# Decay attention and gated convolution on one core: the rows of q, kT and the state are told by the sequence instead of the head's parity

## The chip, the core and the metric

The kernel runs on one core of one Trainium2 chip. The metric is device time in microseconds of one execution; lower is better. A core has TensorE (PE; its weight loads are listed apart as PEld), VectorE (DVE), ScalarE (ACT), GpSimd (POOL) and SyncE (SP), which issues the transfers here. SBUF has 128 partitions; TensorE writes its products to the banks of PSUM.

## The reference

Two layers follow each other. The first is linear attention with a decay `lam` for each head, computed in blocks; the second gates a linear layer by a short causal convolution:

```python
# B=4 sequences, H=8 heads, S=768 tokens, D=64; block = 64
for b in range(nb):
    intra = einsum('bhic,bhjc->bhij', qb, kb) * Dmask       # lam^(i-j) for i >= j, else 0
    intra = einsum('bhij,bhjd->bhid', intra, vb)
    inter = einsum('bhid,bhde->bhie', qb * lam_pow, kv_state)
    out[:, :, sl] = intra + inter
    kv_state = lam_block * kv_state + einsum('bhsd,bhse->bhde', kb * rev_pow, vb)
# x = out as (B, S, 512)
gate = sigmoid(sum_k conv_w[k] * xp[:, k:k+S])              # 5 taps, causal
return (gate * (x @ w_val)) @ w_out
```

`q`, `k`, `v` and `lam` are fp32; `w_val`, `conv_w` and `w_out` come as 64-bit numbers, which the kernel turns into fp32 (the two matrices into pairs of rounded numbers, `_hi` and `_lo`) on the chip.

## The kernel before

The work is cut into twelve steps `i`. A step takes two of the four sequences (`NB2`, index `b`) and 128 tokens (`C`; the decay lets the block be larger than the reference's). Steps 0 to 5 run through the tokens of sequences 0 and 1, steps 6 to 11 through those of 2 and 3. Heads are numbered `h = 2 g + hh`: `g` from 0 to 3, `hh` the parity.

Each step does, in the names of the code:

- `plan_load` (L321): two transfers of 1 MB, one for each sequence, with q and k transposed (`qT`, `kT`: rows are the 64 dimensions of the heads, the upper 64 partitions for even heads and the lower 64 for odd ones) and v and k by tokens.
- `scale_k` (L399): k times the decay to the block's end, on ScalarE for steps in `K_ACT`, else on GpSimd. `scale_q` (L416): q times the decay from the block's start, on GpSimd.
- `scores` (L449) and `mask` (L466), for each `b`: kT times q on TensorE, and the result times `dmask` on VectorE, into `A`. There is one slot of two PSUM banks for scores (`s`); steps in `S_OWN` take two general banks for their second half.
- `inter` (L503): the state times the scaled q, sixteen 64 by 64 products with 128 columns, into `xp` (one slot of two banks, one bank for each `b`). `state[r, b, g, :]` has the rows of its head's parity, and the result goes to the partitions of the same parity, so a product sits on one of two diagonal 64 by 64 tiles of TensorE's array.
- `intra` (L519): v times `A`, added into `xp`.
- `outer` (L560), `update` (L573), `fade` (L579): the new state on TensorE, VectorE and GpSimd.
- `keep` (L619), `split_x` (L641), `split_x_lo` (L649): `xp` to SBUF, and its split into `x_hi` and `x_lo`. For steps in `X_DVE` the split is read from PSUM, with VectorE for `x_lo`.
- once in two steps, for four groups of channels: `tap` (L673), one on ScalarE and four on VectorE, and `sigmoid` (L689).
- `value` (L713), `apply` (L732), `split_h` (L752), `project` (L776), `store` (L792): the two linear layers with weights in two parts. Steps from `DIRECT` on multiply the gate straight from PSUM; earlier ones copy the product to SBUF first.

Steps 9, 10 and 11 (`STACK`) have no `inter`. There the first 64 keys and the state are stacked into one stationary operand of 128 rows (`vs`, filled by a transfer of `vh` and a copy of the state on ScalarE), with the moving operand stacked alike in `A` (half masked scores, half scaled q). The other 64 keys follow in `rest_of_keys` (L542): sixteen 64 by 64 products with 64 columns. Masks there are four VectorE instructions for a half step, and `scale_q` two on GpSimd.

The order on each engine is fixed at build time by `Plan` (L46). Each piece of work is added with an engine, a cost in ns, what it follows, the buffers that it holds and a rank. `Plan.order` simulates the engines, and an engine that is free takes the ready piece with the lowest rank whose buffers have a free slot (`SLOTS`). On TensorE a change of the tile mode costs `SWITCH`, and work of the present mode is preferred by `NEAR`. `RANK` sets how far each stage runs ahead or behind. PSUM has four general banks (`u`), which `value`, `project`, `outer` and the taps' sums share.

Of the kernel before, what the change touches and what calls it, by code (L numbers as in the profile page):

```python
# [9 lines left out]
F32 = mybir.dt.float32  # L10
# [13 lines left out]
SLOTS = {"ld": 3, "qd": 2, "A": 2, "x": 3, "xs": 2, "g": 2, "val": 4, "hs": 2, "o": 2, "s": 1, "xp": 1, "u": 4, "vs": 1}  # L24
UNIT = 2

K_ACT = (0, 1, 2, 3, 4)
X_DVE = (0,)
# [3 lines left out]

STACK = (9, 10, 11)
SWITCH = 130
OVER = {"DVE": 60, "ACT": 85, "POOL": 45}
NEAR = 0.6
# [96 lines left out]
def decay_attention_then_gated_conv(  # L133
# [3 lines left out]
    vh: bass.AP,  # L137
# [7 lines left out]
    B, NC = qkv.shape[0], qkv.shape[1]  # L145
    S = NC * C
    D = P // 2
    NP = qkv.shape[4] // C
    H = 2 * NP
    DM = H * D  # L150
# [6 lines left out]
    UC = HU * P  # L157
    PSUM = bass.MemoryType.PSUM
# [18 lines left out]

    swapped = const.tile([P, P], F32, name="swapped")
    for lo in (0, D):
        nc.gpsimd.tensor_copy(swapped[:, lo : lo + D], ident[:, D - lo : P - lo])  # L180
# [11 lines left out]
    lam_hd = const.tile([P, NP], F32, name="lam_hd")  # L192
# [6 lines left out]
    own_rows = lambda hh: slice(hh * D, (hh + 1) * D)  # L199
    other_rows = lambda hh: slice(D - hh * D, P - hh * D)  # L200
    sdec = const.tile([P, NB2, NP, D], F32, name="sdec")
# [6 lines left out]
    def make_dmask():  # L208
        for hh in range(2):
            for g in range(NP):  # L210
                nc.vector.tensor_tensor_scan(
                    out=dmask[:, hh, g, :],
                    data0=lam_bc[:, 2 * g + hh : 2 * g + hh + 1].to_broadcast([P, C]),
                    data1=ident if hh else swapped,
                    initial=0.0,
                    op0=ALU.mult,
                    op1=ALU.add,
                )

    def make_qdec(g):  # L220
        if g == 0:
            lam_v = lam_bc.rearrange("p (g hh) -> p hh g", hh=2)
            nc.vector.tensor_copy(lam_hd[0:D], lam_v[0:D, 0])
            nc.vector.tensor_copy(lam_hd[D:P], lam_v[D:P, 1])
        nc.vector.tensor_tensor_scan(
            out=qdec[:, g, :],
            data0=lam_hd[:, g : g + 1].to_broadcast([P, C]),
            data1=zero,
            initial=1.0,
            op0=ALU.mult,  # L230
            op1=ALU.add,
        )

    t_dmask = add("DVE", 5500, make_dmask, rank=-4)
# [86 lines left out]
    def plan_load(i):  # L321
        pair, c = divmod(i, NC)
        ld_buf[i] = Buf("ld")
        for b in range(NB2):


            cuts = (0, 2, 4) if i == 0 else (0, 4)
            for lo, hi in zip(cuts, cuts[1:]):

                def go(i=i, lo=lo, hi=hi, b=b, src=qkv[NB2 * pair + b, c]):  # L330
                    if i not in lds:
                        t = buf("ld", "ld", [P, NB2, 4, DM])
                        lds[i] = {
                            "all": t,
                            "qT": t[:, :, 0].rearrange("p b (g i) -> p b g i", g=NP),
                            "kT": t[:, :, 1].rearrange("p b (g i) -> p b g i", g=NP),
                            "v": t[:, :, 2],
                            "k": t[:, :, 3],
                        }
                    nc.sync.dma_start(lds[i]["all"][:, b, lo:hi], src[:, lo:hi])  # L340

                t_ld[i, b, hi] = add(
                    "DMA", 630 * (hi - lo), go, [], [ld_buf[i]],
                    i * RANK["ld"] + 0.01 * b + (-10 + 0.1 * lo if i == 0 else 0), lag=2300,
                )
            t_ld[i, b, 2] = t_ld[i, b, cuts[1]]
# [41 lines left out]
    t_state = t_sdec = t_x = t_vs = None  # L388
    vs = {}
# [3 lines left out]
    for i in range(N):  # L393
# [5 lines left out]
        def scale_k(i=i):  # L399
            kv = lds[i]["k"].rearrange("p b (g hh d) -> p hh g b d", hh=2, d=D)  # L400
            for hh in range(2):
                if i in K_ACT:
                    for g in range(NP):
                        nc.scalar.mul(kv[:, hh, g], kv[:, hh, g], dmask[:, hh, g, C - 1 : C])  # L404
                else:
                    for b in range(NB2):
                        nc.gpsimd.tensor_tensor(
                            out=kv[:, hh, :, b], in0=kv[:, hh, :, b],
                            in1=dmask[:, hh, :, C - 1 : C].to_broadcast([P, NP, D]),
                            op=ALU.mult,  # L410
                        )

        stacked = i in STACK
        A_buf = {b: Buf("A") for b in range(NB2)}

        def scale_q(b, i=i, s=s, stacked=stacked):  # L416
            if stacked:
                s["A", b] = buf("A", "A", [P, 2, NP, C])
                for hh in range(2):
                    r = own_rows(hh)  # L420
                    nc.gpsimd.tensor_tensor(
                        out=s["A", b][r, hh], in0=lds[i]["qT"][r, b], in1=qdec[r], op=ALU.mult
                    )
                return
            if b == 0:
                s["qd"] = buf("qd", "qd", [P, NB2, NP, C])
            nc.gpsimd.tensor_tensor(out=s["qd"][:, b], in0=lds[i]["qT"][:, b], in1=qdec, op=ALU.mult)  # L427

        t_kd = None
        t_qd = {}  # L430
        qd_buf = Buf("qd")
        if not last:
            t_kd = add(
                *(("ACT", 3150) if i in K_ACT else ("POOL", 2500)), scale_k,
                [t_ld[i, 0, 4], t_ld[i, 1, 4], t_dmask], [ld_buf[i]], R + RANK["kd"], port=i not in K_ACT, name=f"kd{i}",
            )
        if not first:
            for b in range(NB2):
                t_qd[b] = add(
                    "POOL", 2550 if stacked else 1300, lambda b=b, f=scale_q: f(b), [t_ld[i, b, 2], t_qdec, t_qd.get(0)],  # L440
                    [ld_buf[i], A_buf[b] if stacked else qd_buf], R + RANK["kd"], port=True, name=f"qd{i}",
                )

        t_mask = {}
        for b in range(NB2):
            own = b == 1 and i in S_OWN
            s_bufs = [Buf("u"), Buf("u")] if own else [Buf("s")]

            def scores(i=i, b=b, s=s, own=own, stacked=stacked):  # L449
                t = lds[i]  # L450
                if own:
                    s["s"] = [bank("so", [P, NP, C]) for hh in range(2)]
                else:
                    sp = bank("s", [P, 2, NP, C], "s")
                    s["s"] = [sp[:, 0], sp[:, 1]]
                    s["sp"] = sp
                for g in range(NP):
                    for hh in range(2):
                        r = slice(hh * D, (hh + 1) * D)
                        nc.tensor.matmul(  # L460
                            s["s"][hh][:, g, :], t["kT"][r, b, g, :], t["qT"][r, b, g, :],
                            start=True, stop=True,
                        )
                s["s", b] = s["s"] if own or stacked else s["sp"]

            def mask(b=b, s=s, own=own, stacked=stacked):  # L466
                if stacked:

                    if "A2" not in s:
                        s["A2"] = buf("qd", "A2", [P, NB2, NP, D])  # L470
                    for hh in range(2):
                        r = other_rows(hh)
                        nc.vector.tensor_tensor(  # L473
                            out=s["A", b][r, hh], in0=s["s", b][hh][r], in1=dmask[r, hh], op=ALU.mult
                        )
                    for hh in range(2):
                        r = own_rows(hh)
                        nc.vector.tensor_tensor(  # L478
                            out=s["A2"][r, b], in0=s["s", b][hh][r, :, D:], in1=dmask[r, hh, :, D:], op=ALU.mult
                        )  # L480
                    return
                s["A", b] = buf("A", "A", [P, 2, NP, C])
                if own:
# [369 lines left out]
```

## Time and profile before

| what | before |
|---|---|
| time, median of 3 runs | 237.28 us (235.39 to 237.3) |
| the profiled execution | 237.42 us, its span 235.6 us |
| TensorE busy | 222.2 us (94%) |
| VectorE, ScalarE, GpSimd busy | 155.5, 120.4, 141.1 us |
| bytes moved | HBM read 30.17 MB, written 6.29 MB |

The span runs from the first to the last instruction. "Busy" is the time in which an engine works on some instruction; the ends of TensorE's records are modelled, so they overlap a little. The chain of waits goes back from the last instruction, at each step to what released it. A timeline row gives start, length, engine, line, operation, operands and how many instructions it merges. One product of fp32 operands makes two records on TensorE and two on PEld.

### The profile page before, as it was taken

To read this page: it belongs to the slowest core of one execution; us is meant where nothing else is said; L and a number is where in the kernel's file an instruction comes from. 1 tells how busy PE (TensorE), PEld (TensorE's weight loads), DVE (VectorE), ACT (ScalarE), POOL (GpSimd) and SP (SyncE) were. 2 spreads that over 40 slices of the span, in tenths; PEclk is the share of its full clock that TensorE was granted. 3 is DMA by queue.
4 is the path that set the end of the run, shared out by engine and by line. 5 is a ranking of instruction groups with operands and counts; after the bars stand their busy time and mean duration, and the time that the engine had idled before them with its cause. 6 is when DMAs were issued, how large, how long until landed. Compare 5 with 4: busy or idle time off the path is not lost.

```text
span 235.6 us, 5414 instructions
## 1 busy us (share of the span) xinstructions
PE 222.2 (94%) x2302; PEld 198.0 (84%) x2302; DVE 155.5 (66%) x211; ACT 120.4 (51%) x200; POOL 141.1 (60%) x120
## 2 busy tenths in 40 slices
PE   7978999889799999999999979999999899999994
PEld 6967789779699999997778869898899799999984
DVE  4777798999998588840899799859811794111110
ACT  2385998735237636653675733866425373322222
POOL 1064899978693796999997946456125243522220
PEclk9999999999999999999999999999999999999999
DMA  5999999987430808009132121110111101111112
GB/s 159 419 420 423 419 419 419 309 312 331 199 161 11 344 18 345 3 13 359 76 92 89 45 89 47 40 53 3 47 45 50 64 22 45 55 62 62 48 46 89
DMA packets 9096, 36.81 MB, mean 156 GB/s; under 512 B 1264, under 2 KB 2288, under 8 KB 5744
## 3 DMA queue, kind: packets, MB, share of 16 engines
q1 hardware_dynamic: 9072, 36.47, 40.0%
q8 instruction: 18, 0.29, 0.5%
q14 instruction: 6, 0.05, 0.1%
HBM read 30.17 MB, written 6.29 MB: 155 GB/s over the span
## 4 chain that ended last, share of the span: by engine, by line
PE 65%; DVE 18%; DMA 8%; ACT 5%; issue 2%; SPq 0%; ACTq 0%; DVEq 0%
PE op L782 28%; PE vp L721 26%; DVE acc L685 9%; DMA ld<-in_qkv 8%; PE s L460 5%; DVE A L489 3%; PE xp L525 3%; DVE g L734 2%; PE xp L510 2%; PE st L567 2%; DVE A L473 1%; ACT ld L404 1%; DVE w_e L257 1%; DVE w_m L290 1%; DVE A L478 1%
## 5 line engine op out<-in xcount | busy, mean ns | idle before, releaser
L685 DVE SCALAR_TENSOR_TENSOR acc<-x,conv_sb,acc 128x512 f32<-128x512 f32 x96 | 66.2, 748 | 2.4 <-ACT acc L683 2.1
L782 PE MATMUL op<-wo_hi,hs 128*128 128x512 f32 (+1 forms) x200 | 61.2, 388 | 0.6 <-ACT g L690 0.5
L721 PE MATMUL vp<-x_hi,wv_hi 128*128 128x256 f32 x192 | 54.7, 285 | 1.4 <-ACT g L690 0.7
L759 POOL TENSOR_TENSOR hs<-g,hs 128x512 fp32r<-128x512 f32 x24 | 31.4, 1309 | 39.7 <-ACT hs L756 36.6
L721 PE MATMUL vp<-x_hi,wv_lo 128*128 128x256 f32 x192 | 53.7, 280 | 0.0
L721 PE MATMUL vp<-x_lo,wv_hi 128*128 128x256 f32 x192 | 53.7, 279 | 0.0
L782 PEld LDWEIGHTS op<-wo_hi,hs 128*128 128x128 f32 x200 | 35.7, 188 | 8.3 <-ACT g L690 1.1
L721 PEld LDWEIGHTS vp<-x_hi,wv_hi 128*128 128x128 f32 x192 | 36.0, 188 | 3.5 <-ACT o L790 1.1
L782 PE MATMUL op<-wo_lo,hs 128*128 128x512 f32 (+1 forms) x100 | 38.6, 386 | 0.0
L721 PEld LDWEIGHTS vp<-x_lo,wv_hi 128*128 128x128 f32 x192 | 36.0, 188 | 0.5
L656 POOL TENSOR_TENSOR x_lo<-x,x_hi 128x1024 fp32r<-128x1024 f32 x11 | 27.7, 2522 | 14.5 <-ACT x_hi L647 14.5
L721 PEld LDWEIGHTS vp<-x_hi,wv_lo 128*128 128x128 f32 x192 | 36.1, 188 | 0.0
L734 DVE TENSOR_TENSOR g<-vp,g 128x512 f32<-128x512 f32 x12 | 8.3, 691 | 40.5 <-PE vp L721 40.5
L460 PE MATMUL s<-ld 64*128 64x128 f32 x352 | 26.5, 292 | 3.9 <-DMA ld<-in_qkv 1.4
L427 POOL TENSOR_TENSOR qd<-ld,qdec 128x512 f32<-128x512 f32 x14 | 19.8, 1422 | 16.3 <-DMA ld<-in_qkv 16.3
L790 ACT COPY o<-op 128x512 f32<-128x512 f32 (+1 forms) x25 | 14.2, 569 | 29.9 <-PE op L782 25.6
L460 PEld LDWEIGHTS s<-ld 64*128 64x128 f32 x352 | 22.3, 194 | 8.0 <-issue 4.2
L489 DVE TENSOR_TENSOR A<-s,dmask 128x1024 f32<-128x1024 f32 x16 | 19.5, 1217 | 8.7 <-PE s L460 7.4
L690 ACT ACTIVATE g<-acc 128x512 f32<-128x512 f32 x24 | 14.3, 598 | 19.8 <-DVE acc L685 19.8
L756 ACT CAST hs<-g 128x512 fp32r<-128x512 f32 x24 | 14.8, 618 | 15.8 <-DVE g L734 15.7
L782 PEld LDWEIGHTS op<-wo_lo,hs 128*128 128x128 f32 x100 | 18.8, 188 | 4.2
L525 PE MATMUL xp<-A,ld 128*64 128x128 f32 x288 | 19.1, 280 | 0.0
(66 smaller groups left out, 312.4 us busy)
## 6 DMA issues: line engine op xcount, KB each, us to landing
ld<-in_qkv SPq DMA_DIRECT2D x22, 1024.0 KB, 8.3
out<-o SPq DMA_DIRECT2D x23, 256.0 KB, 2.0
ld<-in_qkv SPq DMA_DIRECT2D x4, 512.0 KB, 5.8
w_raw<-in_w_val SPq DMA_DIRECT2D x2, 1024.0 KB, 15.6
w_raw<-in_w_out SPq DMA_DIRECT2D x2, 1024.0 KB, 13.8
vs<-in_vh SPq DMA_DIRECT2D x6, 128.0 KB, 3.7
out<-o SPq DMA_DIRECT2D x2, 128.0 KB, 1.7
conv_raw<-in_conv_w SPq DMA_DIRECT2D x1, 20.0 KB, 6.7
```

Of the source, the lines that this page charges most:

```text
L427: nc.gpsimd.tensor_tensor(out=s["qd"][:, b], in0=lds[i]["qT"][:, b], in1=qdec, op=ALU.mult)
L460: nc.tensor.matmul(s["s"][hh][:, g, :], t["kT"][r, b, g, :], t["qT"][r, b, g, :], start=True, stop=True,)
L489: nc.vector.tensor_tensor(out=s["A", b], in0=s["s", b], in1=dmask, op=ALU.mult)
L525: nc.tensor.matmul(s["xp"][hh * D : (hh + 1) * D, b, g, :], vs["t"][:, hh, b, g] if stacked else lds[i]["v"][:, b, h * D : (h + 1) * D], s ...
L656: nc.gpsimd.tensor_tensor(out=s["x_lo"], in0=s["x"], in1=s["x_hi"].bitcast(F32), op=ALU.subtract)
L685: nc.vector.scalar_tensor_tensor(out=to, in0=src, scalar=w, in1=to, op0=ALU.mult, op1=ALU.add)
L690: nc.scalar.activation(xu[un]["g"][:, ct].rearrange("p u (b i) -> p b u i", b=NB2), xu[un]["acc", ct].rearrange("p b (u i) -> p b u i", u= ...
L721: nc.tensor.matmul(vp[:, f, :], w[:, ct, fs], xx[:, ct, :], start=n_mm == 0, stop=n_mm == 3 * NT - 1,)
L756: nc.scalar.copy(s["h_hi"][:, us], gs(u))
L759: nc.gpsimd.tensor_tensor(out=s["h_lo"][:, us], in0=gs(u), in1=s["h_hi"][:, us].bitcast(F32), op=ALU.subtract,)
L782: nc.tensor.matmul(op[:, cols], hh[:, ft, ts], w[:, ft, cols], start=n_mm == 0, stop=n_mm == 3 * NT - 1,)
L790: nc.scalar.copy(s["o", b, j][:, cols], s["op", b, j][:, cols])
```

## The change

In a step, the upper 64 partitions of q, kT and the state now hold the first sequence and the lower 64 the second, for all eight heads; before, they held even and odd heads of either sequence. The half steps of `scores`, `mask` and `intra` are now four heads of both sequences (`u`) instead of all heads of one (`b`). In `inter` the row half is the sequence and the column half is the head's parity. `STACK` with all its parts (`vs`, `vh`, `rest_of_keys`, `swapped`) is gone, so all steps but 0 and 6 have `inter`. The host arranges the inputs to match, and a step's two transfers are now q with kT, and v with k. Several of the planner's numbers differ.

```diff
-DIRECT = 6
+DIRECT = 5
-RANK = {"value": 4.5, "gate": 1.5, "project": 6, "wv": 1.05, "half": 1.1, "wo": 4.5, "ld": 1.0, "kd": -1, "scores": -0.5, "pace": 1, "gpace": 0.95}
+RANK = {"value": 4.5, "gate": 2.5, "project": 7, "wv": 1.05, "half": 1.5, "wo": 4.5, "ld": 0.8, "kd": -1, "scores": -0.5, "pace": 1, "gpace": 0.9}
-K_ACT = (0, 1, 2, 3, 4)
-X_DVE = (0,)
+K_ACT = (0, 1, 2, 3, 4, 6)
+X_DVE = (0, 1)
-STACK = (9, 10, 11)
-NEAR = 0.6
+NEAR = 1
...
-    dmask = const.tile([P, 2, NP, C], F32, name="dmask")
-    qdec = const.tile([P, NP, C], F32, name="qdec")
-    state = const.tile([P, NB2, NP, D], F32, name="state")
+    dmask = const.tile([P, H, C], F32, name="dmask")
+    qdec = const.tile([P, H, C], F32, name="qdec")
+    state = const.tile([P, H, D], F32, name="state")
+    rows = lambda n: slice(n * D, (n + 1) * D)
...
-    for g in range(NP):
-        t_qdec = add("DVE", 400 if g else 800, lambda g=g: make_qdec(g), [t_qdec], rank=0.4)
+    for h in range(H):
+        t_qdec = add("DVE", 400, lambda h=h: make_qdec(h), [t_qdec], rank=0.4)
...
-            cuts = (0, 2, 4) if i == 0 else (0, 4)
+        cuts = (0, 1, 2, 3, 4) if i == 0 else (0, 2, 4)
...
+                    t = buf("ld", "ld", [P, 4, 2, DM])
+                    hd = t.rearrange("p a w (h i) -> p a w h i", h=HP)
+                    lds[i] = {
+                        "all": t, "qT": hd[:, 0:2, 0], "kT": hd[:, 0:2, 1], "v": t[:, 2:4, 0], "k": t[:, 2:4, 1],
+                    }
...
+                for h in range(HP):
+                    for b in range(NB2):
+                        nc.tensor.matmul(
+                            s["s"][b][:, h, :], t["kT"][rows(b), u, h, :], t["qT"][rows(b), u, h, :],
+                            start=True, stop=True,
+                        )
...
-                for pair in (((0, 0), (1, 1)), ((1, 0), (0, 1))):
-                    for g in range(NP):
-                        for hh, b in pair:
-                            r = slice(hh * D, (hh + 1) * D)
-                            nc.tensor.matmul(
-                                s["xp"][r, b, g, :], state[r, b, g, :], s["qd"][r, b, g, :],
+                for g in range(NP):
+                    for hh in range(2):
+                        for b in range(NB2):
+                            h = 2 * g + hh
+                            nc.tensor.matmul(
+                                s["xp"][rows(hh), b, g, :], state[rows(b), h, :], s["qd"][rows(b), h, :],
                                 start=g == 0, stop=False, skip_group_check=True,
...
-            t_from = add("PE", 1900, inter, [t_state, *t_qd.values()], [xp_buf, qd_buf], R, lag=260, mode=2, name=f"in{i}")
+            t_from = add("PE", 950, inter, [t_state, t_qd], [xp_buf, qd_buf], R, lag=260, mode=2, name=f"in{i}")
...
+                for hl in range(HP):
+                    h = HP * u + hl
+                    for b in range(NB2):
                         nc.tensor.matmul(
+                            s["xp"][rows(h % 2), b, h // 2, :],
+                            lds[i]["v"][:, b, h * D : (h + 1) * D],
+                            s["A", u][:, b, hl, :],
...
-            def rest_of_keys(i=i, s=s):
...
+                for h in range(H):
+                    hs = slice(h * D, (h + 1) * D)
+                    for b in range(NB2):
+                        nc.tensor.matmul(
+                            s["st"][rows(b), h, :], lds[i]["k"][:, b, hs], lds[i]["v"][:, b, hs],
                             start=True, stop=True,
                         )
...
-                for b in range(NB2):
-                    nc.gpsimd.tensor_tensor(
-                        out=sdec[:, b], in0=state[:, b],
-                        in1=qdec[:, :, C - 1 : C].to_broadcast([P, NP, D]), op=ALU.mult,
-                    )
+                nc.gpsimd.tensor_tensor(
+                    out=sdec, in0=state, in1=qdec[:, :, C - 1 : C].to_broadcast([P, H, D]), op=ALU.mult
+                )
```

More of the change, by code (lines that the diff above doesn't have):

```diff
@@ L206, in decay_attention_then_gated_conv, with make_dmask, make_qdec @@
     add = plan.add
-    def make_dmask():
-        for hh in range(2):
-            for g in range(NP):
[L211 to L217, printed above, removed]
-                )
[L220 to L224, printed above, removed]
+    def make_dmask(u):
+        for h in range(HP * u, HP * (u + 1)):
+            nc.vector.tensor_tensor_scan(
+                out=dmask[:, h, :],
+                data0=lam_bc[:, h : h + 1].to_broadcast([P, C]),
+                data1=ident,
+                initial=0.0,
+                op0=ALU.mult,
+                op1=ALU.add,
+            )
+    def make_qdec(h):
         nc.vector.tensor_tensor_scan(
-            out=qdec[:, g, :],
-            data0=lam_hd[:, g : g + 1].to_broadcast([P, C]),
+            out=qdec[:, h, :],
+            data0=lam_bc[:, h : h + 1].to_broadcast([P, C]),
             data1=zero,
@@ L232, in make_qdec @@
         )
-    t_dmask = add("DVE", 5500, make_dmask, rank=-4)
+    t_dmask = {u: add("DVE", 2750, lambda u=u: make_dmask(u), rank=-4 + 0.1 * u) for u in range(2)}
     t_qdec = None
-    for g in range(NP):
-        t_qdec = add("DVE", 400 if g else 800, lambda g=g: make_qdec(g), [t_qdec], rank=0.4)
+    for h in range(H):
+        t_qdec = add("DVE", 400, lambda h=h: make_qdec(h), [t_qdec], rank=0.4)
     def widen(after, take, make, n, hi, lo, view, rank):
@@ L323, in plan_load, with go @@
         ld_buf[i] = Buf("ld")
-        for b in range(NB2):
-            cuts = (0, 2, 4) if i == 0 else (0, 4)
[L328 to L346, printed above, removed]
+        cuts = (0, 1, 2, 3, 4) if i == 0 else (0, 2, 4)
+        for lo, hi in zip(cuts, cuts[1:]):
+            def go(i=i, lo=lo, hi=hi, src=qkv[pair, c]):
+                if i not in lds:
+                    t = buf("ld", "ld", [P, 4, 2, DM])
[3 more added lines that the diff above has]
+                    }
+                nc.sync.dma_start(lds[i]["all"][:, lo:hi], src[:, lo:hi])
+            t = add(
+                "DMA", 1260 * (hi - lo), go, [], [ld_buf[i]],
+                i * RANK["ld"] + 0.01 * lo + (-10 + 0.1 * lo if i == 0 else 0), lag=2300,
+            )
+            for part in range(lo, hi):
+                t_ld[i, part] = t
     class Weight:
@@ L399, in scale_k, with scale_q @@
         def scale_k(i=i):
[L400 to L406, printed above, removed]
-                        nc.gpsimd.tensor_tensor(
[L408 to L420, printed above, removed]
+            kv = lds[i]["k"].rearrange("p b (h d) -> p b h d", d=D)
+            if i in K_ACT:
+                for h in range(H):
+                    nc.scalar.mul(kv[:, :, h], kv[:, :, h], dmask[:, h, C - 1 : C])
+            else:
+                for b in range(NB2):
                     nc.gpsimd.tensor_tensor(
-                        out=s["A", b][r, hh], in0=lds[i]["qT"][r, b], in1=qdec[r], op=ALU.mult
+                        out=kv[:, b], in0=kv[:, b], in1=dmask[:, :, C - 1 : C].to_broadcast([P, H, D]), op=ALU.mult
                     )
[L424 to L430, printed above, removed]
+        def scale_q(u, i=i, s=s):
+            if u == 0:
+                s["qd"] = buf("qd", "qd", [P, H, C])
+            hs = slice(HP * u, HP * (u + 1))
+            nc.gpsimd.tensor_tensor(out=s["qd"][:, hs], in0=lds[i]["qT"][:, u], in1=qdec[:, hs], op=ALU.mult)
+        t_kd = t_qd = None
         qd_buf = Buf("qd")
@@ L434, in decay_attention_then_gated_conv @@
                 *(("ACT", 3150) if i in K_ACT else ("POOL", 2500)), scale_k,
-                [t_ld[i, 0, 4], t_ld[i, 1, 4], t_dmask], [ld_buf[i]], R + RANK["kd"], port=i not in K_ACT, name=f"kd{i}",
+                [t_ld[i, 2], t_ld[i, 3], *t_dmask.values()], [ld_buf[i]], R + RANK["kd"], port=i not in K_ACT, name=f"kd{i}",
             )
         if not first:
[L438 to L441, printed above, removed]
-                )
@@ L444, in decay_attention_then_gated_conv, with scores @@
[L444 to L449, printed above, removed]
+            for u in range(2):
+                t_qd = add(
+                    "POOL", 1300, lambda u=u, f=scale_q: f(u), [t_ld[i, u], t_qdec, t_qd], [ld_buf[i], qd_buf], R + RANK["kd"], port=True, name=f"qd{i}",
+                )
+        t_mask, A_buf = {}, {}
+        for u in range(2):
+            own = u == 1 and i in S_OWN
+            s_bufs, A_buf[u] = [Buf("u"), Buf("u")] if own else [Buf("s")], Buf("A")
+            def scores(i=i, u=u, s=s, own=own):
@@ L483, in mask @@
+                s["s", u] = s["s"] if own else s["sp"]
+            def mask(u=u, s=s, own=own):
+                s["A", u] = buf("A", "A", [P, NB2, HP, C])
+                m = dmask[:, HP * u : HP * (u + 1)]
                 if own:
-                    for hh in range(2):
-                        nc.vector.tensor_tensor(
-                            out=s["A", b][:, hh], in0=s["s", b][hh], in1=dmask[:, hh], op=ALU.mult
-                        )
-                else:
-                    nc.vector.tensor_tensor(out=s["A", b], in0=s["s", b], in1=dmask, op=ALU.mult)
@@ L491, in decay_attention_then_gated_conv @@
[L491 to L494 removed]
+                    for b in range(NB2):
+                        nc.vector.tensor_tensor(out=s["A", u][:, b], in0=s["s", u][b], in1=m, op=ALU.mult)
+                else:
+                    nc.vector.tensor_tensor(
+                        out=s["A", u].rearrange("p b h i -> p b (h i)"),
+                        in0=s["s", u].rearrange("p b h i -> p b (h i)"),
+                        in1=m.rearrange("p h i -> p (h i)")[:, None, :].to_broadcast([P, NB2, HP * C]), op=ALU.mult,
+                    )
@@ L495, in decay_attention_then_gated_conv @@
+            t_s = add("PE", 930, scores, [t_ld[i, u]], [ld_buf[i], *s_bufs], R + RANK["scores"], lag=260, mode=1, name=f"s{i}{u}")
+            t_mask[u] = add(
+                "DVE", 1380 if own else 1230, mask, [t_s, t_dmask[u]], [*s_bufs, A_buf[u]], R - 3, name=f"m{i}{u}"
             )
@@ L500, in decay_attention_then_gated_conv @@
         t_from = None
-        if not first and not stacked:
+        if not first:
             def inter(s=s):
                 s["xp"] = bank("xp", [P, NB2, NP, C], "xp")
-                for pair in (((0, 0), (1, 1)), ((1, 0), (0, 1))):
-                    for g in range(NP):
-                        for hh, b in pair:
-                            r = slice(hh * D, (hh + 1) * D)
+                for g in range(NP):
+                    for hh in range(2):
+                        for b in range(NB2):
+                            h = 2 * g + hh
@@ L516, in decay_attention_then_gated_conv, with intra @@
         t_in = []
-        for b in range(NB2):
-            def intra(i=i, b=b, s=s, first=first, stacked=stacked):
-                if (first or stacked) and b == 0:
+        for u in range(2):
+            def intra(i=i, u=u, s=s, first=first):
+                if first and u == 0:
                     s["xp"] = bank("xp", [P, NB2, NP, C], "xp")
-                for g in range(NP):
-                    for hh in range(2):
-                        h = 2 * g + hh
+                for hl in range(HP):
+                    h = HP * u + hl
+                    for b in range(NB2):
@@ L531, in intra @@
+                            s["A", u][:, b, hl, :],
+                            start=first and h < 2, stop=h >= H - 2, skip_group_check=True,
                         )
             t_in.append(
-                add(
-                    "PE", 930, intra, [t_from, t_mask[b], t_ld[i, b, 4], *t_in, t_vs if stacked else None],
-                    [xp_buf, A_buf[b], ld_buf[i], *([vs_buf] if stacked else [])],
-                    R, lag=260, mode=3, name=f"ia{i}{b}",
-                )
-            )
```

126 lines of the change are left out of this document (23 added, 103 removed).

## The prediction

> **What bounds the kernel now.** I read the page first, for the busy shares and the chain that ended last:
>
> ```profile
> span 235.6 us, 5414 instructions
> ...
> PE 222.2 (94%) x2302; PEld 198.0 (84%) x2302; DVE 155.5 (66%) x211; ACT 120.4 (51%) x200; POOL 141.1 (60%) x120
> ...
> PE 65%; DVE 18%; DMA 8%; ACT 5%; issue 2%; SPq 0%; ACTq 0%; DVEq 0%
> PE op L782 28%; PE vp L721 26%; DVE acc L685 9%; DMA ld<-in_qkv 8%; PE s L460 5%; DVE A L489 3%; PE xp L525 3%; DVE g L734 2%; PE xp L510 2%; PE st L567 2%; DVE A L473 1%; ACT ld L404 1%; DVE w_e L257 1%; DVE w_m L290 1%; DVE A L478 1%
> ```
>
> TensorE is busy for 94% of the span and carries 65% of the chain. The rest of the chain is VectorE, DMA and ScalarE. Where those parts lie is told by busy time in stretches (columns: the stretch, its length, then busy time and instructions of PE, PEld, DVE, ACT, POOL, then granted clock, DMA share, GB/s):
>
> ```profile
> 0.00:20.00 20.00, 17.26 (x220) 15.86 (x222) 12.81 (x31) 9.35 (x24) 5.12 (x14) 1.00 0.90 345
> 20.00:40.00 20.00, 18.28 (x281) 16.03 (x279) 17.02 (x17) 18.61 (x38) 17.83 (x13) 1.00 1.01 418
> 40.00:63.00 23.00, 19.97 (x326) 17.98 (x322) 23.00 (x28) 11.87 (x17) 20.27 (x19) 1.00 0.78 284
> 63.00:105.00 42.00, 41.66 (x522) 39.48 (x524) 33.02 (x36) 21.92 (x29) 32.85 (x26) 1.00 0.36 142
> 105.00:140.00 35.00, 34.33 (x278) 27.77 (x273) 25.67 (x35) 20.30 (x34) 29.64 (x27) 1.00 0.33 121
> 140.00:187.00 47.00, 45.51 (x404) 40.31 (x404) 30.78 (x49) 23.51 (x38) 21.38 (x15) 1.00 0.13 47
> 187.00:235.60 48.60, 45.19 (x288) 40.56 (x288) 13.18 (x20) 14.85 (x25) 14.03 (x10) 1.00 0.14 55
> ```
>
> From 63 us on TensorE idles 0.34 + 0.67 + 1.49 us up to 187 us, and 3.41 us in the stretch that holds the kernel's end. From 20 to 63 us it idles 1.72 + 3.03 = 4.75 us, and there another engine is full: ScalarE 18.61 of 20 us, then VectorE 23.00 of 23. So after 63 us each microsecond taken off TensorE comes off the span; before it, only if the planner finds other products to put there. All TensorE idle from 20 to 187 us is 4.75 + 2.50 = 7.25 us.
>
> **The change, part by part.** *The state's products.* Next the chain in order of time, for what each kind of TensorE step adds when it runs back to back (start, length, record count):
>
> ```profile
> 81.37 1.89 PE xp L510 x32
> 83.26 1.09 PE s L460 x16
> 84.35 1.02 PE xp L525 x16
> 85.38 0.93 PE st L567 x32
> 86.31 0.88 PE xp L525 x16
> ```
>
> and two answers of the timeline for the first of them, with the product that stands in its place in the last steps:
>
> ```profile
> 81.30 0.33 PE L510 MATMUL xp<-qd,state 64*64 64x128 f32 x2
> ...
> 81.30 1.96 PE L510 MATMUL xp<-qd,state 64*64 64x128 f32 x32
> ...
> 118.79 1.15 PE L548 MATMUL xp<-A,ld 64*64 64x64 f32 x32
> ```
>
> ```profile
> L510 PE MATMUL xp<-qd,state x224: 269/269/320, 16.6 to 98.6; 64*64 64x128 f32 x112
> ```
>
> `inter` has 16 products and 32 records, so an fp32 product is two records. The first two records together last 0.33 us, and one lasts up to 0.32 (the row above, min/median/max in ns): they start within some 0.01 us. The two halves of one product share weights' rows and columns of the array, so these are the first halves of two products on two tiles. The other 15 pairs add (1.96 - 0.33) / 15 = 0.109 us each. So two tiles run at once, a pair of records each 0.109 us; 16 pairs are 1.74 us and the rest of 1.89 is entry and exit. The changed loop (sequence innermost, then head parity) names four different tiles in four products. If all four run, 32 records are 8 rounds of 0.109 instead of 16, which takes 8 x 0.109 = 0.87 us off: 1.89 becomes 1.02. Four at once is not in the trace. What is: two tiles side by side that share no rows or columns (this step), two that share all columns (`s`, 16 records 1.09), two that share all rows (`xp` L525, 16 records 0.88 to 1.02). Below, the bound is 0 saved; above, 0.87. I take 0.87, because every pairing of the four exists by itself at full speed. How often and where:
>
> ```profile
> 20.00:63.00 43.00, 7.86 (x128) 1.00 0.89 347
> 63.00:105.00 42.00, 3.93 (x64) 1.00 0.36 142
> ```
>
> (the same stretches view for L510 alone): 4 + 2 of the seven steps that have `inter` (all but the two first of a pair and the three last); one lies before. The saving is 7 x 0.87 = 6.1 us of TensorE time, 1.7 of it where TensorE is the bound, 3.5 in the crowded 43 us, 0.9 at the start.
>
> *Steps 9 to 11* lose `rest_of_keys` and get `inter`. The former spans 1.15 us, the latter by the same reckoning 0.33 + 7 x 0.109 = 1.09: nothing for TensorE. Their other engines gain (rows by tile: count, min/median/max ns, first and last start):
>
> ```profile
> L489 DVE TENSOR_TENSOR A<-s,dmask x16: 1209/1218/1226, 7.9 to 88.8; 128x1024 f32<-128x1024 f32 x16
> L473 DVE TENSOR_TENSOR A<-s,dmask x12: 682/688/695, 101.0 to 159.1; 64x512 f32<-64x512 f32 x12
> L478 DVE TENSOR_TENSOR A<-s,dmask x12: 403/416/427, 102.3 to 160.1; 64x256 f32<-64x256 f32 x12
> ...
> L581 POOL TENSOR_TENSOR sdec<-state,qdec x16: 612/619/1609, 16.5 to 127.3; 128x256 f32<-128x256 f32 x16
> L427 POOL TENSOR_TENSOR qd<-ld,qdec x14: 1268/1287/2276, 12.3 to 71.3; 128x512 f32<-128x512 f32 x14
> L421 POOL TENSOR_TENSOR A<-ld,qdec x12: 1257/1294/1309, 105.3 to 144.6; 64x512 f32<-64x512 f32 x12
> L225 DVE TENSOR_TENSOR_SCAN qdec<-lam_hd,zero x4: 416/420/424, 6.3 to 11.6; 128x128 f32<-128x128 f32 x4
> ```
>
> Six stacked masks of 2 x 0.69 + 2 x 0.42 = 2.21 us become six of 1.22 (VectorE -5.9 us); twelve half-height `scale_q` of 1.29 become six of 1.29 (GpSimd -7.8); the six state copies on ScalarE and six transfers of `vh` go. From 105 us on all this lies beside a TensorE that is full, with one exception that the timeline shows:
>
> ```profile
> 138.76 1.39 DVE L473 TENSOR_TENSOR A<-s,dmask 64x512 f32<-64x512 f32 x2
> 140.07 0.84 DVE L478 TENSOR_TENSOR A<-s,dmask 64x256 f32<-64x256 f32 x2
> ...
> 141.02 0.38 PE L460 MATMUL s<-ld 64*128 64x128 f32 x2 [1.19 <-issue]
> ```
>
> The second half's scores wait 1.19 us, and start 0.1 us after the mask has left the only scores bank. A mask shorter by 2.21 - 1.22 = 1.0 us releases it 1.0 us sooner. I take -1.0; what is then late is at most the 0.2 that remains.
>
> *The first products with v* (`intra`) are reordered too, and unsaid by the title. Before, the column half alternates with each product; after, two products in a row (both sequences) go to the same half. Bounds: 0 if the second tile's product may pass the waiting one, up to one product's two records, 2 x 0.109 = 0.22 us, at the start of each of 24 groups: 5.2 us. I take 0: in the pair of 0.01 us above, a product had already passed the waiting second half of the one before it.
>
> *Loads.* The same two transfers a step,
>
> ```profile
> ld<-in_qkv SPq DMA_DIRECT2D x22, 1024.0 KB, 8.3
> ```
>
> but q with kT of both sequences first, v with k second. The scores of both halves get their data with the first; the first `intra` now needs the second. One such transfer at the 418 GB/s of 20 to 40 us is 2.5 us: between -2.5 and +2.5 there, hidden elsewhere by three load buffers. I take 0, as the two signs stand in the same step.
>
> *VectorE constants:* `qdec` is eight scans of 0.42 instead of four (+1.7, less two tiny copies), in the first 20 us where VectorE is busy 12.81: covered; where it isn't, 1.7. *`X_DVE` with step 1* takes a subtraction off GpSimd and gives VectorE one over the same bank as a mask, so about 1.22; the bank of `xp` is held until it is over. Today a ScalarE copy of
>
> ```profile
> 25.93 1.00 ACT L623 COPY x<-xp 128x1024 f32<-128x1024 f32 x1
> ```
>
> releases it; another such copy and the subtraction can put `inter` of step 2 off by 1.0 + 1.2 = 2.2 us. Between 0 and 2.2 I take 0, since `inter` there wins back 0.87 and TensorE has other products queued; both ends stay in the range. *`K_ACT` with 6* moves two to four GpSimd products to eight ScalarE ones at about 70 us, where ScalarE is busy 21.92 of 42; *`DIRECT` 5* lets step 5 skip two ScalarE copies; `fade` becomes one instruction of about 1.29 instead of 2 x 0.62. Zero each, beside a full TensorE. *New ranks:* the order changes throughout; its price is the change of TensorE's 7.25 us of gaps. Apart from the 1.0 above I take 0.
>
> The sum, against the profiled execution's 237.42 us (span 235.6 and 1.8 around it, and within 0.1% of the median of 237.28): 237.42 - 6.1 - 1.0 = 230.3. I say 230.5.
>
> **Rivals.** *The crowded stretch keeps its length.* From 20 to 63 us VectorE or ScalarE is nearly full, so four savings may only lengthen TensorE's idle time: 3.5 us lost, 233.8. If moreover VectorE's added 1.22 and 1.7 land there, 236.7. For it: VectorE's 23.00 of 23. Against: once `wv` is widened TensorE has value products that can go there, and later taps (gate rank 2.5 for 1.5) unload VectorE.
>
> *`intra` pays for its order:* 235.5, worked out above. Against it speaks the order in the middle of the present `inter`: its second half begins with the tile that the first half ended on, and the 15 pairs still leave no pause of 0.22.
>
> *Slower: the tiles don't run four at a time.* The third and fourth tile share rows with the first two. If their weights can't be loaded while those stream, `inter` stays at 1.89 and now runs in ten steps: 10 x 1.89 - (7 x 1.89 + 3 x 1.08) = +2.4 us, 1.08 being L548's 1.15 less the overlap of 0.07 that 1.96 has over 1.89. That is 239.8, or 238.8 with the shorter masks; it decides once less than 0.24 us of the 0.87 is won per step. Against: `intra`'s two tiles share all 128 rows, and its 16 records take 0.88, which is eight pairs of 0.109.
>
> The Trainium skill, "TensorE: Matmul & The Clock Gate", section "Part 3: Packing small matmuls — row/col tiling", states just this rule: weight loads overlap with running products only when the row group differs. By it this rival would hold; `intra`'s rows so far contradict it.
>
> **Numbers.** Forecast 0.62: 230.5, by gaps that halve or grow by 3 us, 226.8 to 233.3. Crowded stretch 0.14 (half still faster by 1%, half not). `intra` 0.09 (0.8% faster, so within 1%). No four tiles 0.09: at the edge of 1%, a third within, two thirds beyond, as gaps may grow with it. Fewer gaps than half 0.06. A measurement of this kernel can tell about 1% from no change, 2.4 us. Faster 0.62 + 0.06 + 0.07 = 0.75; within 1% 0.07 + 0.09 + 0.03 = 0.19; slower 0.06. The range 226.5 to 236 reaches a little past 226.8 and 235.5; it leaves out the 0.06 with few gaps, the 0.09 without four tiles and about 0.03 at the first rival's far end.
>
> **What would show it.** Right: an `inter` of 32 records spans 1.1 us, ten of them; `intra` still 0.9 to 1.0 per 16 records; PE busy near 216; no 1.2 us gap before a late `s`. Wrong: `inter` at 1.9 (no four tiles), `intra` at 1.1 to 1.3 (order), or TensorE idle above 8 us between 20 and 63 us.

## The result, and the profile after

The changed kernel takes 231.88 us (median; before 237.24): 0.9765 of the time before, 95% interval 0.9741 to 0.979, or 5.6 us less. Its profiled execution took 231.06 us with a span of 229.3; before, 237.42 and 235.6. The forecast was 230.5, by a sum of 230.3 against that profiled execution. Where a median and a ratio below seem not to fit, the ratio is the one to read: it leaves disturbed runs out.

The page of the changed kernel, busy shares and the chain that ended last:

```profile
span 229.3 us, 5368 instructions
...
PE 215.6 (94%) x2302; PEld 191.2 (83%) x2302; DVE 149.9 (65%) x196; ACT 117.4 (51%) x200; POOL 124.4 (54%) x91
...
PE 68%; DVE 16%; DMA 10%; ACT 3%; issue 1%; SPq 0%; ACTq 0%; DVEq 0%
```

TensorE is busy for 6.6 us less and the span is 6.3 us shorter, so nearly all of the work saved came off the end, and TensorE's idle time is the same in sum: 13.4 us before, 13.7 after. It moved, though. The same stretches as in the prediction (same columns; the last one ends with the span):

```profile
0.00:20.00 20.00, 15.84 (x220) 14.20 (x222) 13.13 (x32) 8.88 (x24) 4.77 (x11) 0.91 0.89 333
20.00:40.00 20.00, 16.63 (x291) 14.62 (x287) 16.32 (x17) 17.88 (x35) 15.88 (x10) 1.00 1.02 421
40.00:63.00 23.00, 21.28 (x356) 18.75 (x353) 23.00 (x32) 15.41 (x28) 17.02 (x13) 1.00 0.82 315
63.00:105.00 42.00, 42.00 (x535) 39.19 (x534) 35.78 (x35) 23.84 (x31) 33.41 (x23) 1.00 0.46 172
105.00:140.00 35.00, 34.58 (x346) 29.20 (x345) 30.27 (x40) 17.71 (x29) 25.88 (x19) 1.00 0.12 47
140.00:187.00 47.00, 46.01 (x331) 40.62 (x330) 27.95 (x42) 23.45 (x39) 17.44 (x11) 1.00 0.12 46
187.00:229.30 42.30, 39.23 (x240) 34.58 (x238) 3.46 (x5) 10.19 (x18) 10.02 (x7) 1.00 0.16 63
```

From 20 to 63 us TensorE idles 3.37 + 1.72 = 5.09 us (before 4.75), from 63 to 187 us 0 + 0.42 + 0.99 = 1.41 (before 2.50), and in the first 20 us 4.16 (before 2.74).

The chain in order of time shows the products that were changed:

```profile
76.09 1.09 PE s L426 x16
77.18 1.03 PE xp L463 x32
78.22 1.08 PE st L496 x32
79.30 0.92 PE xp L478 x16
80.22 0.93 PE st L496 x30
81.16 0.88 PE xp L478 x16
```

`inter` (L463) adds 1.03 us for its 32 records, where it added 1.89. `scores` (L426) and `intra` (L478) are as they were. Three answers of the timeline, for the start of an `inter` (products and weight loads that start before 93.10 us) and for all of it:

```profile
93.02 0.34 PE L463 MATMUL xp<-qd,state 64*64 64x128 f32 x4
93.02 0.21 PEld L463 LDWEIGHTS xp<-qd,state 64*64 64x64 f32 x8
...
93.02 1.10 PE L463 MATMUL xp<-qd,state 64*64 64x128 f32 x32
```

Four records together last 0.34 us, and one of them 0.32: four tiles start within 0.02 us. The other seven rounds add (1.10 - 0.34) / 7 = 0.109 us each, the figure that a round of two had.

### The profile page after: what moved, and what is told of

Its sections match the earlier page's. It is cut to its first block, busy times and chain, and to the rows that moved or that the text cites. A ratio compares the mean times of both kernels' runs of the same rounds, so it can differ in the third digit from the quotient of the medians.

```text
span 229.3 us, 5368 instructions
## 1 busy us (share of the span) xinstructions
PE 215.6 (94%) x2302; PEld 191.2 (83%) x2302; DVE 149.9 (65%) x196; ACT 117.4 (51%) x200; POOL 124.4 (54%) x91
## 4 chain that ended last, share of the span: by engine, by line
PE 68%; DVE 16%; DMA 10%; ACT 3%; issue 1%; SPq 0%; ACTq 0%; DVEq 0%
PE op L686 28%; PE vp L625 28%; DMA ld<-in_qkv 10%; DVE acc L589 7%; PE s L426 4%; PE xp L478 4%; DVE A L439 4%; PE xp L463 2%; DVE w_m L277 1%; PE st L496 1%; ACT ld L385 1%; DVE g L638 1%; DVE w_m L250 1%; DVE state L505 1%; ACT g L594 1%
## 5 line engine op out<-in xcount | busy, mean ns | idle before, releaser
L663 POOL TENSOR_TENSOR hs<-g,hs 128x512 fp32r<-128x512 f32 x24 | 31.9, 1342 | 29.3 <-ACT hs L660 29.2
L560 POOL TENSOR_TENSOR x_lo<-x,x_hi 128x1024 fp32r<-128x1024 f32 x10 | 24.2, 2419 | 33.4 <-ACT x_hi L551 33.4
L638 DVE TENSOR_TENSOR g<-vp,g 128x512 f32<-128x512 f32 x14 | 9.7, 690 | 43.7 <-PE vp L625 34.9
L396 POOL TENSOR_TENSOR qd<-ld,qdec 128x512 f32<-128x512 f32 x20 | 26.5, 1333 | 20.1 <-DMA ld<-in_qkv 20.1
L439 DVE TENSOR_TENSOR A<-s,dmask 128x1024 f32<-128x1024 f32 x22 | 26.8, 1217 | 5.7 <-PE s L426 5.3
L426 PE MATMUL s<-ld 64*128 64x128 f32 x352 | 25.6, 284 | 4.9 <-DMA ld<-in_qkv 2.6
L426 PEld LDWEIGHTS s<-ld 64*128 64x128 f32 x352 | 21.4, 187 | 9.1 <-DVE A L439 3.6
L478 PE MATMUL xp<-A,ld 128*64 128x128 f32 x384 | 27.6, 283 | 0.3 <-DMA ld<-in_qkv 0.3
L478 PEld LDWEIGHTS xp<-A,ld 128*64 128x64 f32 x384 | 22.5, 140 | 2.6 <-issue 0.7
L385 ACT ACTIVATE ld<-ld,dmask 128x128 f32<-128x128 f32 x48 | 14.7, 389 | 11.4 <-DMA ld<-in_qkv 11.3
```

The source lines that it names most:

```text
L385: nc.scalar.mul(kv[:, :, h], kv[:, :, h], dmask[:, h, C - 1 : C])
L396: nc.gpsimd.tensor_tensor(out=s["qd"][:, hs], in0=lds[i]["qT"][:, u], in1=qdec[:, hs], op=ALU.mult)
L426: nc.tensor.matmul(s["s"][b][:, h, :], t["kT"][rows(b), u, h, :], t["qT"][rows(b), u, h, :], start=True, stop=True,)
L439: nc.vector.tensor_tensor(out=s["A", u].rearrange("p b h i -> p b (h i)"), in0=s["s", u].rearrange("p b h i -> p b (h i)"), in1=m.rearrang ...
L478: nc.tensor.matmul(s["xp"][rows(h % 2), b, h // 2, :], lds[i]["v"][:, b, h * D : (h + 1) * D], s["A", u][:, b, hl, :], start=first and h < ...
L560: nc.gpsimd.tensor_tensor(out=s["x_lo"], in0=s["x"], in1=s["x_hi"].bitcast(F32), op=ALU.subtract)
```

## The experiments

The main theory was that four tiles at once free TensorE of 0.87 us in each `inter`, and that this time comes off the end because TensorE is the bound. The rivals: that the gain comes from the shorter masks and the missing transfers of the stacked steps, or from the planner's new numbers.

### Two tiles at a time

The order of the sixteen products alone is changed; the order of work on every engine stays.

```diff
-                for g in range(NP):
-                    for hh in range(2):
-                        for b in range(NB2):
+                for pair in (((0, 0), (1, 1)), ((1, 0), (0, 1))):
+                    for g in range(NP):
+                        for hh, b in pair:
```

> The changed kernel, with only the order of the sixteen products of inter changed: first the two tiles (first sequence, even heads) and (second sequence, odd heads) in turn, then the other two, so that two tiles that share neither rows nor columns run at a time, as before the change. Every engine's order of work stays. Theory (four tiles at once are the gain): inter spans 1.96 us again instead of 1.10, so ten steps take 10 x 0.87 = 8.7 us more of TensorE; the five of them after 90 us fall on a full TensorE, so the time is 4.3 to 8.7 us above the changed kernel's 231.9, 236 to 240.5. Rival (the gain comes from shorter masks and the new ranks, the four tiles being hidden): inter may be longer but the time stays within 1.5 us of 231.9. Rival (tiles were never four at a time, the order doesn't matter): inter stays at 1.10.

Measured: 234.44 us, 0.99 of before (0.9866 to 0.9933), so 0.0135 x 237.3 = 3.2 us more than the changed kernel. That is more than the rival's 1.5 us and less than the theory's 4.3, since `inter` grew less than was reckoned, from 1.10 to 1.59 us instead of 1.96. Six answers of this run's timeline tell why. Each takes in the products of one `inter` that start up to a later and later time, and its length runs to the end of the last of them:

```profile
94.83 0.33 PE L463 MATMUL xp<-qd,state 64*64 64x128 f32 x2
...
94.83 0.65 PE L463 MATMUL xp<-qd,state 64*64 64x128 f32 x8
...
94.83 0.76 PE L463 MATMUL xp<-qd,state 64*64 64x128 f32 x10
...
94.83 0.87 PE L463 MATMUL xp<-qd,state 64*64 64x128 f32 x14
...
94.83 1.15 PE L463 MATMUL xp<-qd,state 64*64 64x128 f32 x24
...
94.83 1.59 PE L463 MATMUL xp<-qd,state 64*64 64x128 f32 x32
```

The first ten records go two to a round (0.33 + 4 x 0.109 = 0.77). Between 0.87 and 1.15 us ten more end in 0.28, about four to a round. The last eight take 0.44, two to a round again. The profile doesn't name the tile of a record, but two tiles alone can't make four to a round. So the third and fourth tile take up their products when ten of the sixteen records of the first two have started: products of different tiles pass each other. Ten steps x 0.49 = 4.9 us of TensorE gave 3.2 us of time, by the two intervals combined between 2.2 and 4.2.

### `inter` done twice

```diff
-                for g in range(NP):
-                    for hh in range(2):
+                for g, hh in [(g, hh) for _ in range(2) for g in range(NP) for hh in range(2)]:
+                    if True:
                         for b in range(NB2):
```

> The changed kernel with inter's sixteen products done twice, one after the other (the second time over the first). The order of all other work stays. With four tiles at once the second time costs 8 x 0.109 = 0.87 us, so a step has about the 1.89 us that it had on two tiles. Theory (the four tiles are the whole gain): ten steps x 0.87 = 8.7 us of TensorE, of which, as with the diagonal order (4.9 us of TensorE gave 3.2), about two thirds reach the end: time 231.9 + 5.8 = 237.7, ratio to before near 1.0. Rival (the shorter masks and transfers hold a part of their own): 234.5 or less.

Measured: 1.0073 of before (1.0029 to 1.0116), median 240.17. `inter` adds 1.91 us in the chain, for 64 records:

```profile
82.29 1.91 PE xp L463 x64
```

So ten steps x 0.88 = 8.8 us of TensorE cost 0.0308 x 237.3 = 7.3 us of time (by the intervals combined 6.1 to 8.5), five sixths of it where two thirds were reckoned. The whole gain of 5.6 us is undone, and more, by giving `inter` back its old length. The rival that masks and transfers carry a part of it asked for 234.5 or less, and falls; what the planner's numbers carry is asked below.

### No stacked steps in the kernel before

```diff
-STACK = (9, 10, 11)
+STACK = ()
```

> The kernel before with STACK empty: its last three steps have inter on two tiles like the others and no larger products. Theory: TensorE takes 3 x (1.89 - 1.08) = 2.4 us more, and the shorter masks take 1.0 us of its gaps: time 237.2 + 1.4 = 238.6, between 237.5 and 240. Rival (the stacked steps cost more by their masks and copies than they save on TensorE): 236.5 or less.

Measured: 238.36 us, 1.0045 of before (1.003 to 1.006), 1.1 us more where 1.4 was reckoned. The stacked products were a gain as long as `inter` went on two tiles. With `inter` at 1.03 us, against the 1.08 that the prediction reckoned for `rest_of_keys`, they should have nothing to offer; no run has them on the new rows.

### The rows and the numbers apart

Both arrangements were run with the other's planner numbers: the new rows with RANK, NEAR, DIRECT, K_ACT and X_DVE of before,

> The new arrangement of rows with all of the planner's numbers as before the change (RANK, NEAR, DIRECT 6, K_ACT without 6, X_DVE with step 0 alone). Theory (the rows carry the gain): inter 1.10, PE busy near 216, time 231 to 234. Rival (the numbers carry a good part): PE busy also falls but its gaps grow, time 235 or more.

and the old rows with the new numbers (the stacked steps kept).

> The old arrangement, with stacked last steps, and the new planner's numbers. Theory (the rows carry the gain): PE busy stays at 222, time 236 to 239. Rival (the numbers carry a good part): 234 or less.

Measured: 238.66 us, 1.0051 of before (1.0022 to 1.008), for the first; 239.4 us, 1.009 (1.0075 to 1.0105), for the second. The second went the theory's way (TensorE busy 221.9 us, the time 0.4 above its range): the new numbers alone gain nothing. The first went by its rival: TensorE's work fell and its gaps grew, and the new rows alone lose the whole gain. Its page and its stretch from 140 us:

```profile
span 237.4 us, 5348 instructions
...
PE 219.0 (92%) x2302; PEld 193.3 (81%) x2302; DVE 146.9 (62%) x195; ACT 116.3 (49%) x194; POOL 129.7 (55%) x94
...
140.00:187.00 47.00, 43.21 (x360) 37.33 (x360) 23.63 (x35) 20.64 (x33) 14.91 (x10) 0.96 0.09 35
```

TensorE has 237.4 - 219.0 = 18.4 us of gaps, against 13.7 with the new numbers, 3.8 of them in the late stretch where the changed kernel has 1.0. It is also busy for 3.4 us longer with the same products. The granted clock of 0.96 in that stretch doesn't account for it, since over the whole span the mean clock is 0.993 in both executions; what does wasn't traced. So the time that four tiles free is there, and the order of the work decides whether it reaches the end.

### Which numbers

Five runs take single numbers of the changed kernel back. The ranks and NEAR together:

> The changed kernel with RANK and NEAR as before the change. Theory (with the old ranks TensorE runs out of ready products, since projections are not held back): most of the 6.8 us between the changed kernel and the one with all old numbers comes back, time 236 to 239, with TensorE idle between 140 and 187 us. Rival (the loss came from the engines' numbers): 231 to 234.

The engines' numbers together (K_ACT without step 6, X_DVE with step 0 alone, DIRECT 6), and X_DVE alone:

> The changed kernel with K_ACT, X_DVE and DIRECT as before the change. Theory (ranks matter, these don't): 231 to 234, and inter of step 2 starts earlier, since the 1.7 us wait for VectorE's x_lo is gone. Rival: 236 or more.

> The changed kernel with X_DVE holding step 0 alone. TensorE's order is then the one of the run with all three engine numbers old. Theory (that order, which puts no value product between 35 and 50 us, made that run slow): time 240 to 244, with scores waiting for masks for 8 us or more and the granted clock under 0.9 between 40 and 63 us. Rival (K_ACT or DIRECT made it slow; X_DVE costs the 1.7 us for which inter waits on x_lo): 230 to 232.

The projections' rank, and the gates' rank:

> The changed kernel with the projections' rank 6 in place of 7. Theory (holding projections back keeps TensorE in work later on): half or more of the 5.3 us that the old ranks cost, 234 to 237, with new gaps after 105 us. Rival (another rank did it): 231 to 233.

> The changed kernel with the gates' rank 1.5 in place of 2.5, so that the taps come earlier on VectorE. Theory (later taps unload VectorE between 20 and 63 us): 233 to 237, with masks later and more TensorE idle before 63 us. Rival: 231 to 233.

| taken back | ratio to before (95%) | against the changed kernel |
|---|---|---|
| nothing (the changed kernel) | 0.9765 (0.9741 to 0.979) | |
| RANK and NEAR | 0.9985 (0.9961 to 1.001) | +5.2 us |
| K_ACT, X_DVE, DIRECT | 1.0236 (1.0158 to 1.0313) | +11.2 us |
| X_DVE alone | 1.0248 (1.0193 to 1.0303) | +11.5 us |
| "project" 6 alone | 0.9918 (0.9892 to 0.9944) | +3.6 us |
| "gate" 1.5 alone | 1.0044 (1.0022 to 1.0067) | +6.6 us |

(The last column is the difference of the ratios times 237.3.) The medians are 237.22, 242.98, 244.23, 236.05 and 238.94 us. The ranks and the projections' rank came within what was expected, the gates' rank cost 2 us more than that: TensorE's gaps grew from 5.1 to 6.2 us between 20 and 63 us, as expected, but from 0.4 to 3.8 between 105 and 140. The expectation for the engines' numbers missed: it had them harmless; that for X_DVE alone, written after it, held.

The two runs with step 0 alone in X_DVE have an order that a usable kernel can't have. The second pair of sequences begins with a copy into `state` (L503), and the planner isn't told that this copy must follow the last `inter` of the first pair, which still reads the old state. In these two orders it comes ahead of it. VectorE's copy of step 6 and TensorE's `inter` of step 5:

```profile
61.45 0.68 DVE L503 COPY state<-st 128x512 f32<-128x512 f32 x1
...
66.13 1.10 PE L463 MATMUL xp<-qd,state 64*64 64x128 f32 x32
```

This is the fifth of the run's ten `inter`. It reads the state of the wrong sequences, so neither run computes the reference. The amount of work is the same, so their times show what such an order costs, not what X_DVE is worth in a kernel that computes the reference. In the changed kernel the `inter` starts at 51.05 us and the copy at 59.87.

With X_DVE as before, a part of the kernel goes like this on TensorE (its stretches: length, PE busy, granted clock, DMA share, GB/s):

```profile
34.00:42.00 8.00, 5.44 (x96) 1.00 1.03 410
42.00:51.00 9.00, 5.63 (x65) 0.56 0.86 350
51.00:63.00 12.00, 12.00 (x162) 0.90 0.01 3
```

while the changed kernel has

```profile
34.00:42.00 8.00, 8.00 (x137) 1.00 1.01 415
42.00:51.00 9.00, 7.55 (x135) 1.00 0.95 360
```

and the timeline of the slower one says what TensorE waited for:

```profile
42.58 1.60 PE L426 MATMUL s<-ld 64*128 64x128 f32 x16 [2.89 <-DVE A L439]
46.38 2.08 PE L426 MATMUL s<-ld 64*128 64x128 f32 x16 [2.19 <-DVE A L439]
49.05 1.97 PE L496 MATMUL st<-ld 128*64 128x64 f32 x32 [0.59 <-ACT g L594]
```

In that order no value product stands between 35 and 50 us; scores follow scores, each waiting for a mask to free the one scores bank, and with TensorE idle the granted clock is down to 0.56 in the second stretch. In the changed kernel the first value products are put at 35 us. Which of the planner's comparisons tipped it there wasn't traced.

The projections' rank shows the same thing later on. With rank 6 (first fence), and with 7:

```profile
149.00:154.30 5.30, 3.40 (x65) 1.00 0.00 2
154.30:159.00 4.70, 4.67 (x25) 0.64 0.00 0
```

```profile
149.00:154.30 5.30, 5.30 (x85) 1.00 0.14 53
154.30:159.00 4.70, 4.70 (x29) 1.00 0.04 16
```

With rank 6 the projections are used up by 149 us, TensorE has nothing beside the gates' waits, idles 1.9 us and then works at 0.64 of the clock. With 7 there is a reserve.

### The order in `intra`

The column half alternates with each product, as before the change:

```diff
-                for hl in range(HP):
-                    h = HP * u + hl
-                    for b in range(NB2):
+                for hl, b in [(2 * p + hh, b) for p in range(HP // 2) for b in range(NB2) for hh in range(2)]:
+                    h = HP * u + hl
+                    if True:
```

> The changed kernel with intra's products in an order in which the column half alternates with each product, as before the change; the order of all other work stays. Theory (a product passes those that wait for another tile): no change, 16 records still span 0.88 to 1.07 us, time within 0.4% of the changed kernel's. Rival (two products in a row on one half cost at the start of a group): up to 24 x 0.22 = 5.2 us less of TensorE and 2 to 5 us less time.

Measured: 231.16 us, 0.9723 of before (0.9671 to 0.9776); the intervals overlap, so no difference is shown in time, as the theory had it. In the chain of the alternating run and of the changed kernel, two groups of `intra` in a row, in this order:

```profile
131.62 1.90 PE xp L478 x32
```

```profile
131.03 1.95 PE xp L478 x32
```

The changed order costs about 0.05 us at the entry to `intra`, not 0.22.

### A longer warm-up

The last run adds four warm-up products (`WARM` 13) to the alternating order.

> The changed kernel with intra's alternating order and 13 warm-up products instead of 9, so that TensorE has no pause before the first scores even when the first transfer lands at 6.6 us. Theory (the start is bound by transfers, and only the clock gains): the granted clock is 1.0 in the first 20 us in every run, the time 230.5 to 231.5 with less spread. Rival (the products delay the first scores): 232 or more.

Measured: 231.27 us, 0.9732 of before (0.9707 to 0.9757): the same as without. The granted clock of its profiled execution is 1.00 in the first 20 us, where the changed kernel's is 0.91; but the alternating run without the extra products has 1.00 there too, so the run doesn't show what a better clock at the start is worth. The times didn't lie closer together, as was expected: they go from 230.92 to 234.96. The first scores start at 6.46 us, with 9 warm-up products at 6.54, so these products delay nothing. No run beat the changed kernel by more than the measurement can tell.

## Why the prediction was right

**Four tiles at once, 0.87 us for each `inter`.** Right to a hundredth: 1.03 for a reckoned 1.02, in ten steps. The step that took 0.87 rather than 0, since each pairing of tiles ran at full speed by itself, held; four of them together do too. The rival that ended slower is refuted by the four records within 0.34 us: the third and fourth tile share rows with the first two, and their weights were loaded all the same. Even the next four loads start before 93.10 us (the row with x8), while the first four products run until 93.36 and both row halves are taken. The rule of the Trainium skill ("TensorE: Matmul & The Clock Gate", section "Part 3: Packing small matmuls — row/col tiling"), that weight loads overlap with running products only when the row group differs, does not hold for these tiles. The section of the Trainium skill also lets a load go ahead into a background weight buffer; no run here tells whether that is what happens. The same section of the Trainium skill has products start strictly in order; the run with two tiles at a time shows the third and fourth tile starting ahead of products that come earlier in the program.

**The saving reaches the end.** Right. TensorE lost 6.6 us of work for 7 x 0.86 = 6.0 in `inter` and 3 x 0.05 in the last steps (the other 0.4 wasn't traced), and the span 6.3 us. Two runs that add time to `inter` and leave the order as it is put figures on it: about two thirds of it reach the end in one, five sixths in the other.

**Shorter masks, 1.0 us.** The wait that it was reckoned from is gone. After 63 us scores wait for a mask once, for 0.32 us, where the longest wait was 1.19:

```profile
129.87 1.16 PE L426 MATMUL s<-ld 64*128 64x128 f32 x16 [0.32 <-DVE A L439]
```

TensorE's gaps from 105 to 187 us went from 0.67 + 1.49 to 0.42 + 0.99 us, 0.75 less. In the kernel before without stacked steps, which has the short masks on the old rows, they are 0.85. No run isolates the mask in the changed kernel.

**The crowded stretch keeps its length.** It didn't: four savings of 0.86 lie there, and TensorE's gaps from 20 to 63 us grew by 0.34, where the rival had 3.5.

**`X_DVE`, between 0 and 2.2 us, taken as 0.** The wait is there, as described, and was not free:

```profile
29.76 1.10 PE L463 MATMUL xp<-qd,state 64*64 64x128 f32 x32 [1.73 <-DVE x_lo L555]
```

This is a good part of the 1.65 us by which the gaps from 20 to 40 us grew. What step 1 in `X_DVE` is worth in all stays open: the run without it is 11.5 us slower, but by an order that reads the wrong state.

**Loads, taken as 0, and the first 20 us.** These cost 1.42 us of gaps that weren't in the sum. The first scores, which wait for the first transfer, start at 6.60 us instead of 5.76. That is no accident of one execution: in all eleven traces with the new rows they start between 6.42 and 6.77 us, in the three with the old rows between 5.71 and 5.82. From 4 to 5 us the transfers move 221 GB/s with a DMA share of 1.01, where they moved 356 with 0.95 (the answers for this microsecond of the changed kernel, then of the kernel before):

```profile
4.00:5.00 1.00, 1.00 (x6) 1.00 1.01 221
```

```profile
4.00:5.00 1.00, 1.00 (x6) 1.00 0.95 356
```

So the new arrangement costs about 0.8 us at the start. Why it is slower there, and how much of it reaches the end, stays open. The eight scans for `qdec` lie beside transfers, as reckoned.

**New ranks, taken as 0.** The sum came out, 13.7 us of gaps for 13.4, but as a balance of parts: 1.42 more in the first 20 us, 0.34 more up to 63, 1.09 less up to 187 and 0.34 less at the end. And the step was weaker than the prediction made it. It took the change of the gaps as small, with bounds of 3 us. With the old numbers the gaps come to 18.4 us and TensorE is busy 3.4 us longer, and the time is 238.66: outside the forecast's own bounds. The gain needed the new numbers, and the prediction worked out nothing that told whether they would fit. That this term came out near 0 was luck.

**`intra`'s order, taken as 0.** Nearly: 0.05 us a group, about a quarter of the upper bound, and not resolved in the time.

## What to carry to other kernels

When small products are limited by the tile that they sit on, arrange the operands so that consecutive products name all tiles: a step of sixteen products that ran on two tiles went from 1.89 us to 1.03 by that alone, and a more involved way around it (stacked operands) could go. In a kernel whose order is fixed by a planner, freed time on the bounding engine shows up only if the planner still has work to put there: re-rank after such a change, and judge it by the engine's gaps in each stretch rather than by its busy time. A new order can also break a dependence that the planner was never told of, as the copy into `state` shows: such dependences have to be written into the plan before it is re-ranked.

## What the runs showed of the hardware

Products on different 64 by 64 tiles pass each other for several places in the program: two tiles at a time, in the order of the first experiment, gave 1.59 us and not 1.96, since the later tiles started after ten of the sixteen records of the first two.

The granted clock can fall without a complete pause. With the projections' rank 6, TensorE was busy for 1.48 of the 3.41 us before it fell, and worked at half the clock for the next 3.41:

```profile
151.18:154.59 3.41, 1.48 (x36) 1.00 0.00 0
154.59:158.00 3.41, 3.41 (x18) 0.50 0.00 0
```

In the run with the old numbers it was 1.64 of 3.41, followed by 0.50 as well. Shorter gaps left the clock alone: 2.24 us busy of 3.41 in the changed kernel, from 18.61 us on, with the clock at 1.00 there and in the 20 us after. Where the line lies wasn't measured. A gap on TensorE can so cost more than its length: 3.41 us at half the clock are 1.7 us of products' time (an estimate from these rows), nearly as much again as the 1.9 us of the gap.
